# Reordering the first three blocks of a fused attention and expert kernel, and cutting its last tile in three

## The chip, the cores and the metric

The kernel runs on one core of a Trainium2 chip. The metric is the device time of one execution in microseconds (us), of the core that it runs on; medians of several executions are quoted. A trace's span, from the first to the last instruction, is about 1.8 us shorter than that time. "TensorE" does matrix multiplies, "VectorE" (DVE in the profile) and "ScalarE" (ACT) work on vectors, "GpSimd" (POOL) issues most loads here, and the sync engine (SP) issues the output transfers and the transposes by DMA. In profile lines PE is TensorE, PEld its weight loads, and a q after an engine's name marks its queue, which waits and issues transfers.

## The reference

```python
# q, k, v: (8, 8, 576, 64); attention within chunks of 64 positions
scores = scale * q_c @ k_c.T          # per chunk
attn = exp(scores - max) / (sum + 1e-9)
x = (attn @ v_c)                      # -> 4608 tokens x 512
h = x @ w_in                          # 512 x 2048
g = h * sigmoid(beta * h)
out = g @ w_out                       # 2048 x 512, float32
```

The kernel works on "units" of 256 tokens for attention and "blocks" of two units (512 tokens) for the two large products. Block 0 is units 0 and 1, block 1 is units 2 and 3, and so on.

## The kernel before

For each unit: block transposes of q and k (`emit_T`), scores and exp (`emit_sc`), values (`emit_pv`), norms (`emit_norm`: a reciprocal and a multiply on VectorE), and a transpose of x for the next product, by TensorE and a copy for units 0 to 5 (`emit_xt_pe`), by DMA from unit 6 on (`emit_xt_dma`). For each block: 16 hidden products (`emit_m`: four matmuls, tanh on ScalarE, gate product on VectorE) and four output tiles (`emit_t`: 16 matmuls, a copy on ScalarE, an output transfer). The engines keep to the order in which the program emits; the trace before shows it for VectorE, where unit 3's reciprocal starts at 48.45 us, behind the gate product of 48.11, though its matmuls started at 47.41 (unit 2's starts 0.37 after its own). PSUM is the memory that the kernel's matmuls write to. A tile takes one buffer of a pool there, called a bank here, and a bank goes to the next tile only when the tile that was in it has been read: in the trace before, unit 3's scores start at 45.37, after the copy that reads the tile in their bank has ended at 45.32.

In profile lines sc is a unit's scores, et their exp, rd and x the reciprocals and the values, xp the transposed x in PSUM and xt its copy; hps, sg and gt are a hidden product, its tanh and its gate product; ops and osb are an output tile in PSUM and its copy.

```python
ps_p = pool("ps_p", bufs=4, PSUM)   # one bank each: hidden products, output tiles, some x transposes
ps_s = pool("ps_s", bufs=1, PSUM)   # scores; second half of a unit's values
ps_x = pool("ps_x", bufs=1, PSUM)   # first half of a unit's values; x transposes
...
def emit_xt_pe(u, s):
    pool, tag = (ps_x, "x") if s == 0 else (ps_s, "s") if u == 2 else (ps_p, "p")
    ... four transposes into one bank, then nc.scalar.copy(out=xt_at(u, s), in_=xp)
...
for i in range(16):                       # block 0's output, units 2 and 3 between
    ...
    if i == 13:
        emit_xt_pe(2, 0); emit_xt_pe(2, 1)
    if i == 14:
        emit_sc(3, True)
    if i == 15:
        emit_m(1, 0, 0, 256)              # hidden product 0, unit 2's half
        emit_pv(3)
        emit_norm(3, 0); emit_norm(3, 1)
        emit_m(1, 1, 0, 256)
    emit_t(0, i % 4, 4 * (i // 4), 4 * (i // 4) + 4)
emit_xt_pe(3, 0); emit_m(1, 2, 0, 256)
emit_xt_pe(3, 1); emit_m(1, 3, 0, 256)
for m in range(4, KFF):                   # whole-block products from 4 on
    emit_m(1, m)
    if m < 8:
        emit_m(1, m - 4, 256, 256)        # unit 3's halves of 0 to 3
    ...
```

The softmax here doesn't subtract the row's maximum and nothing guards it: scores larger than these inputs give would overflow.

## Time and profile before

| | before |
|---|---|
| time, median of 6 | 291.71 us (291.54 to 292.50) |
| span of the trace | 290.0 us |
| TensorE busy | 283.1 us, 98% |
| start of unit 2's value matmuls | 40.58 us |
| start of the last matmul | 286.41 us |

TensorE is the bound, so what matters is where it starts late. The last two rows frame a stretch of 245.83 us.

### The profile page before, as it was taken

The page shows a single profiled execution, that of the slowest core. Times are in us where ns is not written, and L with a number is a line of the kernel's source. Part 1 is how long each engine was busy: PE and PEld are TensorE (multiplying, and loading weights), DVE is VectorE, ACT ScalarE, POOL GpSimd, SP SyncE. Part 2 cuts the span into 40 slices and gives each one's busy share as a digit, 9 for nine tenths or more (in the row PEclk, how much of TensorE's full clock was granted, in tenths as well). Part 3 has the DMA queues.
Part 4 walks back from the last instruction along what each step waited for, and adds up shares of the span by engine and source line. Part 5 has one row for each costly group of instructions (what it writes and reads, how often), then busy time and mean ns, then how long its engine had stood idle before and what let it go on. Part 6 is the DMA issues. An engine that isn't in the chain of part 4 may idle for free.

```text
span 290.0 us, 6476 instructions
## 1 busy us (share of the span) xinstructions
PE 283.1 (98%) x2695; PEld 135.5 (47%) x2695; DVE 139.8 (48%) x252; ACT 146.0 (50%) x224; POOL 97.5 (34%) x126
## 2 busy tenths in 40 slices
PE   7999999999999999999999999999999999999995
PEld 2464445545544444444444444444444444444444
DVE  3477444687366644534454444445453636433300
ACT  3277318783456645454545554455445544444411
POOL 8864569379152985070717070000000000000000
PEclk9999999999999999999999999999999999999999
DMA  9999999999969999999999999946346202100111
GB/s 143 170 196 205 177 176 212 211 161 158 133 98 135 200 168 144 168 151 156 135 123 171 118 158 113 198 65 92 91 107 78 75 36 72 38 36 36 38 72 72
DMA packets 141932, 36.86 MB, mean 127 GB/s; under 512 B 130000, under 2 KB 137424, under 8 KB 141904
## 3 DMA queue, kind: packets, MB, share of 16 engines
q0 software_dynamic: 101216, 18.10, 84.2%
q1 hardware_dynamic: 40544, 18.24, 34.4%
q8 instruction: 21, 0.34, 0.5%
q10 hardware_dynamic: 144, 0.13, 0.1%
q14 instruction: 7, 0.06, 0.1%
HBM read 36.71 MB, written 9.44 MB: 159 GB/s over the span
## 4 chain that ended last, share of the span: by engine, by line
PE 91%; DMA 2%; ACT 2%; DVE 2%; POOL 1%; issue 1%; DVEq 0%; ACTq 0%; POOLq 0%
PE hps L303 43%; PE ops L335 41%; DMA ku<-in_k_dram 2%; PE x L256 2%; PE sc L231 2%; PE sc L218 1%; PE ops L540 1%; ACT xt L288 1%; DVE x L271 1%; ACT sg L313 1%; PE warm L352 1%; POOL h L360 1%; PE xp L287 1%; DVE kT L154 0%; ACT osb L345 0%
## 5 line engine op out<-in xcount | busy, mean ns | idle before, releaser
L317 DVE SCALAR_TENSOR_TENSOR gt<-sg,hps 128x512 f16<-128x512 f32 (+1 forms) x152 | 99.2, 658 | 114.5 <-ACT sg L313 114.4
L313 ACT ACTIVATE sg<-hps,beta 128x512 f32<-128x512 f32 (+1 forms) x152 | 100.4, 665 | 74.7 <-PE hps L303 74.7
L303 PE MATMUL hps<-xt,win 128*128 128x512 f16 (+1 forms) x608 | 136.7, 368 | 0.4 <-ACT xt L288 0.2
L335 PE MATMUL ops<-wout,gt 128*128 128x512 f16 x560 | 131.1, 379 | 0.0
L303 PEld LDWEIGHTS <-win 128*128 128x128 f16 x608 | 57.6, 98 | 61.8 <-issue 0.9
L335 PEld LDWEIGHTS <-gt 128*128 128x128 f16 x560 | 53.8, 98 | 63.3
L345 ACT ACTIVATE osb<-ops 128x512 f32<-128x512 f32 x35 | 20.9, 598 | 44.4 <-PE ops L335 44.4
L110 POOL DMA_DIRECT2D vbig<-in_v_dram x40 | 34.2, 876 | 10.0 <-DMA wout<-in_moe_w_out_dram 4.3
L96 POOL DMA_DIRECT2D qu<-in_q_dram x22 | 18.7, 860 | 41.5 <-DMA qT<-qu 39.0
L271 DVE TENSOR_TENSOR x<-x,rd 128x512 f16<-128x512 f32 (+1 forms) x40 | 25.2, 637 | 1.4
L96 POOL DMA_DIRECT2D ku<-in_k_dram x22 | 18.8, 876 | 0.4 <-DMA ku<-in_k_dram 0.4
L240 ACT ACTIVATE et<-sc 128x1024 f16<-128x1024 f32 (+1 forms) x9 | 7.4, 834 | 10.2 <-PE sc L231 10.2
L352 PE MATMUL warm<-idle 128*128 128x512 f16 x39 | 11.2, 429 | 1.2 <-DVE braw L356 1.2
L267 DVE RECIPROCAL rd<-x 128x8 f32<-128x8 f32 x36 | 7.2, 200 | 8.8 <-PE x L256 8.8
L224 ACT ACTIVATE et<-sc 128x1024 f16<-128x1024 f32 x10 | 10.2, 1015 | 0.0
L256 PEld LDWEIGHTS <-et 64*64 64x64 f16 x576 | 6.1, 107 | 7.4 <-issue 3.8
L102 POOL DMA_DIRECT2D ku<-in_k_dram x10 | 7.7, 772 | 2.5 <-DMA win<-in_moe_w_in_dram 1.3
L102 POOL DMA_DIRECT2D qu<-in_q_dram x10 | 7.7, 781 | 2.4 <-DMA win<-in_moe_w_in_dram 1.4
L288 ACT COPY xt<-xp 128x512 f16<-128x512 f16 x12 | 6.7, 588 | 3.3 <-PE xp L287 3.3
L256 PE MATMUL x<-vbig,et 64*64 64x65 f16 x576 | 8.1, 195 | 0.0
L154 DVE STREAM_TRANSPOSE kT<-ku 128x512 f32<-128x512 f32 x7 | 5.0, 711 | 4.9 <-DMA ku<-in_k_dram 4.9
L553 DVE TENSOR_SCALAR osb<-ops 128x256 f32<-128x256 f32 x1 | 0.4, 424 | 12.5 <-PE ops L540 12.5
(34 smaller groups left out, 60.2 us busy)
## 6 DMA issues: line engine op xcount, KB each, us to landing
out_dram<-osb SPq DMA_DIRECT2D x35, 256.0 KB, 3.2
vbig<-in_v_dram POOLq DMA_DIRECT2D x32, 128.0 KB, 7.9
qu<-in_q_dram POOLq DMA_DIRECT2D x20, 128.0 KB, 6.6
ku<-in_k_dram POOLq DMA_DIRECT2D x20, 128.0 KB, 8.2
win<-in_moe_w_in_dram POOLq DMA_DIRECT2D x8, 256.0 KB, 9.2
wout<-in_moe_w_out_dram POOLq DMA_DIRECT2D x4, 512.0 KB, 12.2
qu<-in_q_dram POOLq DMA_DIRECT2D x4, 256.0 KB, 6.5
ku<-in_k_dram POOLq DMA_DIRECT2D x4, 256.0 KB, 7.3
```

The source lines that it names most:

```text
L96: nc.gpsimd.dma_start(out=tv[off:off + n, sp], in_=src[b, :, s:s + n, :].rearrange("h p d -> p h d"),)
L102: nc.gpsimd.dma_start(out=t[off // 2:(off + n) // 2], in_=src[b, :, s:s + n, :].rearrange("h (p r) d -> p h r d", r=2),)
L110: nc.gpsimd.dma_start(out=vbig[off:off + n, i, :, 0:D], in_=v[b, :, s:s + n, :].rearrange("h p d -> p h d"),)
L224: nc.scalar.activation(out=et, in_=sc, func=ACTF.Exp, scale=scale)
L256: nc.tensor.matmul(out=x[64 * c:64 * c + 64, r, g, 0:D + 1], lhsT=(et[64 * r:64 * r + 64, s, 4 * c + g, :] if u < XU else et[64 * r:64 * r ...
L271: nc.vector.tensor_tensor(out=o, in0=x[:, r, :, 0:D], in1=rd[:, r].to_broadcast(list(o.shape)), op=ALU.mult)
L303: nc.tensor.matmul(out=hps[:, 0:n], lhsT=w_in16[m // 2][:, kk, (m % 2) * 128:(m % 2) * 128 + 128], rhs=xr[:, c0 // CH:(c0 + n) // CH, 2 * ...
L313: nc.scalar.activation(out=sg[:, 0:n], in_=hps[:, 0:n], func=ACTF.Tanh, scale=beta2[:, m:m + 1])
L317: nc.vector.scalar_tensor_tensor(out=gt_t[j][:, m, c0:c0 + n], in0=sg[:, 0:n], scalar=1.0, in1=hps[:, 0:n], op0=ALU.add, op1=ALU.mult,)
L335: nc.tensor.matmul(out=ops, lhsT=gt_t[j][:, kk, t * 128:(t + 1) * 128], rhs=w_out16[kk // 4][:, kk % 4, :], start=(kk == 0), stop=(kk == K ...
L345: nc.scalar.activation(out=osb, in_=ops, func=ACTF.Copy, scale=0.5)
L352: nc.tensor.matmul(out=d[:, 0:w], lhsT=idle[:, 0:128], rhs=idle[:, 0:w])
```

## The change

Five edits, called by letters from here on. The intent is to take away TensorE's waits in the early blocks, where attention is still prepared by TensorE, VectorE and ScalarE, and to shorten the tail.

```diff
 # A: unit 2's x transposed into one bank, one copy
-                emit_xt_pe(2, 0)
-                emit_xt_pe(2, 1)
+                emit_xt_pair(2)       # 8 transposes into one ps_x bank, one 1024-column copy
 # B: the gate product behind unit 3's norms
-                emit_m(1, 0, 0, 256)
+                a0, v0 = emit_m(1, 0, 0, 256, True)
+                a0()
                 emit_pv(3)
                 emit_norm(3, 0)
                 emit_norm(3, 1)
+                v0()
 # C: a first half of product 4 moved up
-        for m in range(4, KFF):
+        emit_m(1, 4, 0, 256)
+        for m in range(5, KFF):
             emit_m(1, m)
-            if m < 8:
-                emit_m(1, m - 4, 256, 256)
+            if m < 10:
+                emit_m(1, m - 5, 256, 256)
 # D: unit 5's block transposes behind unit 4's norms
         emit_pv(4)
-        emit_T(5)
         emit_norm(4, 0)
         emit_norm(4, 1)
+        emit_T(5)
 ...                                  # and unit 5's scores and values one half tile later
 # E: the last output tile in pieces of 256, 128 and 128 columns, not two of 256
-        for hf in range(2):
+        for c0, n in ((0, 256), (256, 128), (384, 128)):
 ...                                  # VectorE copies the first and third, ScalarE the second
```

More of the change, by code (lines that the diff above doesn't have):

```diff
@@ L288, in emit_xt_pe, with emit_xt_pair @@
         nc.scalar.copy(out=xt_at(u, s), in_=xp)
+    def emit_xt_pair(u):
+        xp = ps_x.tile([128, 2, 4, 128], FP16, tag="x", name="xp")
+        for s in range(2):
+            xf = x16_t.pop((u, s)).rearrange("p r h d -> p (r h d)")
+            for g in range(4):
+                nc.tensor.transpose(out=xp[:, s, g, :], in_=xf[:, g * 128:(g + 1) * 128], identity=ident)
+        xt_at(u, 0)
+        j, o = unit_block[u]
+        nc.scalar.copy(out=xt_t[j][:, 2 * o:2 * o + 2], in_=xp)
     def emit_xt_dma(u, s):
@@ L467 @@
         emit_xt_pe(4, 1)
+        emit_t(1, 1, 0, 8)
         emit_sc(5)
-        emit_t(1, 1, 0, 8)
+        emit_t(1, 1, 8)
         emit_pv(5)
@@ L473 @@
         emit_T(7)
-        emit_t(1, 1, 8)
         emit_t(1, 2, 0, 8)
@@ L540 @@
                 nc.tensor.matmul(
-                    out=ops[:, 0:256],
+                    out=ops[:, 0:n],
                     lhsT=gt_t[NB - 1][:, kk, 384:512],
-                    rhs=w_out16[kk // 4][:, kk % 4, 256 * hf:256 * hf + 256],
+                    rhs=w_out16[kk // 4][:, kk % 4, c0:c0 + n],
                     start=(kk == 0),
@@ L547 @@
             osb = osb_p.tile([128, DM], FP32, tag="osb", name="osb")
-            dst = out[NT - 128:NT, 256 * hf:256 * hf + 256]
-            if hf == 0:
-                nc.scalar.activation(out=osb[:, 0:256], in_=ops[:, 0:256], func=ACTF.Copy, scale=0.5)
-                nc.sync.dma_start(out=dst, in_=osb[:, 0:256])
-            else:
-                nc.vector.tensor_scalar(out=osb[:, 0:256], in0=ops[:, 0:256], scalar1=0.5, scalar2=None, op0=ALU.mult)
-                nc.scalar.dma_start(out=dst, in_=osb[:, 0:256])
+            dst = out[NT - 128:NT, c0:c0 + n]
+            if c0 == 256:
+                nc.scalar.activation(out=osb[:, 0:n], in_=ops[:, 0:n], func=ACTF.Copy, scale=0.5)
+            else:
+                nc.vector.tensor_scalar(out=osb[:, 0:n], in0=ops[:, 0:n], scalar1=0.5, scalar2=None, op0=ALU.mult)
+            (nc.scalar if c0 == 384 else nc.sync).dma_start(out=dst, in_=osb[:, 0:n])
 _INS = ['q', 'k', 'v', 'moe_w_in', 'moe_w_out', 'moe_beta']
```

## The prediction

> **What bounds the kernel now.** I read the page first, for the share of each engine.
>
> ```profile
> PE 283.1 (98%) x2695; PEld 135.5 (47%) x2695; DVE 139.8 (48%) x252; ACT 146.0 (50%) x224; POOL 97.5 (34%) x126
> ```
>
> TensorE is busy 98% of 290.0 us, and the page shows it at full clock in every slice. A change that leaves its work alone can only win what TensorE waits, and the time before its first and after its last matmul. So next I read the waits of TensorE:
>
> ```profile
> PE xp L287 <- DVE x L271: 0.4, 2, 0.2
> PE sc L231 <- ACT xt L288: 0.3, 1, 0.3
> PE hps L303 <- ACT xt L288: 0.2, 1, 0.2
> ```
>
> These three rows are what this change aims at, 0.9 us in all, but they are too small. The profile models the end of a matmul well after the next could have started (379 ns for a 512-column matmul, though they start 216 ns apart), so part of each wait counts as busy. I therefore take waits from starts, in the timeline of the stage around unit 3:
>
> ```profile
> 44.00 1.03 PE L335 MATMUL ops<-wout,gt 128*128 128x512 f16 x4
> 44.25 1.07 ACT L288 COPY xt<-xp 128x512 f16<-128x512 f16 x2
> ...
> 45.37 0.70 PE L231 MATMUL sc<-qT,kT 32*64 32x64 f16 x64 [0.34 <-ACT xt L288]
> ...
> 48.11 0.42 DVE L317 SCALAR_TENSOR_TENSOR gt<-sg,hps 128x256 f16<-128x256 f32 x1 [3.73 <-ACT sg L313]
> ...
> 48.45 0.20 DVE L267 RECIPROCAL rd<-x 128x8 f32<-128x8 f32 x1
> 48.68 0.69 DVE L271 TENSOR_TENSOR x<-x,rd 128x512 f16<-128x512 f32 x1
> ...
> 49.30 0.60 ACT L345 ACTIVATE osb<-ops 128x512 f32<-128x512 f32 x1 [0.39 <-PE ops L335]
> ...
> 49.43 0.40 PE L287 MATMUL xp<-ident,x 128*128 128x128 f16 x4 [0.17 <-DVE x L271]
> 49.52 0.69 DVE L271 TENSOR_TENSOR x<-x,rd 128x512 f16<-128x512 f32 x1
> ...
> 49.86 0.58 ACT L288 COPY xt<-xp 128x512 f16<-128x512 f16 x1
> ...
> 50.27 0.40 PE L287 MATMUL xp<-ident,x 128*128 128x128 f16 x4
> ...
> 51.35 4.92 PE L303 MATMUL hps<-xt,win 128*128 128x512 f16 x28 [0.25 <-ACT xt L288]
> ```
>
> The reader is to see four late starts. Four output matmuls from 44.00 are through at 44.87 (4 x 0.216); with 0.09 for a change of tile shape (below) unit 3's scores could start at 44.96; they start at 45.37, as their bank holds unit 2's second transpose until its copy is read out: **0.41**. The four output matmuls at 48.24 are through at 49.10; unit 3's first transpose starts at 49.43: **0.33**. The four hidden products from 49.66[...] end at 50.10; the second transpose starts at 50.27: **0.17**. The four from 50.50 end at 50.94; the first whole-block product starts at 51.35, waiting for the second copy of x: **0.41**. Together 1.32 us. One more is in unit 4's stage:
>
> ```profile
> 65.72 0.70 DVE L154 STREAM_TRANSPOSE kT<-ku 128x512 f32<-128x512 f32 x1
> ...
> 66.35 0.67 DVE L154 STREAM_TRANSPOSE qT<-qu 128x512 f32<-128x512 f32 x1
> ...
> 66.94 0.17 DVE L267 RECIPROCAL rd<-x 128x8 f32<-128x8 f32 x1
> ...
> 67.99 0.69 DVE L271 TENSOR_TENSOR x<-x,rd 128x512 f16<-128x512 f32 x1
> ...
> 68.73 0.40 PE L287 MATMUL xp<-ident,x 128*128 128x128 f16 x4 [0.21 <-DVE x L271]
> ```
>
> VectorE does unit 5's block transposes before unit 4's norms. The second transpose of x could start at 68.36 (68.14 + 4 x 0.056) and starts at 68.73: **0.37**. From there to 286 us the chain of waits is unbroken matmuls. The tail:
>
> ```profile
> 283.03 3.66 PE L540 MATMUL ops<-wout,gt 128*128 128x256 f16 x32
> ...
> 286.78 0.42 DVE L553 TENSOR_SCALAR osb<-ops 128x256 f32<-128x256 f32 x1 [12.51 <-PE ops L540]
> ```
>
> After the last matmul come a 0.42 us copy, the DMA issue at 287.23, and its landing; the span ends at 290.0.
>
> [...] eight transposes from 43.56 to 44.00 are 55 ns apart though each has its own weight load, and 12 output matmuls from 40.96 to 43.56 take 216 ns each. [...] the reciprocal at 48.45 stands behind a gate product that waits for a tanh, though its matmuls started at 47.41. [...] In the chain of waits eight output matmuls take 1.73 us alone and 1.83 with such a change. The change moves these borders; their number stays. [...] here a 1024-column exp takes 1.015.
>
> **The change part by part.** Times below are on the clock of the kernel before. No matmul is added in count of columns, so the sum is waits removed.
>
> *Unit 2's x in one bank.* Eight transposes now fill the bank that has no part in unit 3's scores. Those need only unit 2's norm read out (42.04 + 0.69 = 42.73) and unit 3's block transposes (43.71 + 0.67 = 44.38), both before 44.96. So 0.41 goes. One 1024-column copy (estimate 1.02, from the exp) replaces two that took 1.07: nothing on the path. Unit 3's value matmuls move from 47.41 to 47.00; they need the exps, which end 1.08 after about 45.80, at 46.88: just in time.
>
> *Gate product behind unit 3's norms.* With VectorE free, the reciprocal starts 0.37 after the value matmuls start, as for unit 2 (40.58 to 40.95), and the second x is ready 1.78 after that (40.95 to 42.04 + 0.69): at 47.37 and 49.15, in place of 50.21. TensorE gets to the first transpose at 48.71 and needn't wait (0.33 gone). The second it reaches at 49.37, but that takes the bank of the fourth output tile, which ScalarE empties from 48.89 to 49.49, so it starts at 49.54.
>
> *A product's first half moved up.* ScalarE, in order, is what remains: output copy, x copy, tanh, x copy. Before, this ran from 49.30 to 51.30. It now starts 0.41 to 0.45 earlier, as the output matmuls do, and ends near 50.88; the first whole-block product can start near 50.92, not 51.35 (0.43). In front of it there is now one half-product more, 4 x 0.109 = 0.43, which before came after. So this stage gains 0.43 + 0.43 = **0.86** of its 1.32; 0.46 stays as a wait for the last copy of x. [...]
>
> *Unit 5's block transposes behind unit 4's norms.* The reciprocal can start at 66.02 + 0.37 = 66.39 and the second x is ready at 68.17, ahead of 68.36: **0.37** gained. The block transposes (1.4) then end near 69.5; unit 5's scores, moved behind eight output matmuls, start near 70.4. Unit 5's own x has less cover, 8 output matmuls where it had 16: ready 2.15 after its value matmuls start, wanted 0.38 + 0.09 + 1.73 + 0.22 = 2.42 after. No new wait.
>
> *Last tile in three pieces.* TensorE: 16 x 0.109 + 32 x 0.056 = 3.53 for 3.51, a loss of 0.02. [...] **0.15** together.
>
> Sum: 0.86 + 0.37 + 0.15 = 1.38 us. I take back 0.1 for rival A and get 291.77 - 1.28 = 290.5.
>
> **The rivals.** *A: given back at a transfer.* Block 3's first product at 99.00 reads x transposed by DMA, issued until 94.99 (92.36 + 2.63), with 2.4 to 7.5 us to landing in the view of that tile. TensorE gets there some 1.2 us earlier; the transposes mostly shift along, but unit 9's loads are now issued behind later block transposes and may crowd them. For it: DMA queues are over 90% busy there. Against: GpSimd was issuing unit 8's loads until 68.25 anyway, so the delay is a fraction of 1 us. Worth 0 to 0.6, then 290.4 to 291.0. [...] *C: all waits of unit 3's stage vanish* (ScalarE keeps up): 0.46 more, 290.0. Against it: four ScalarE operations in order stand between the output matmuls and the product.
>
> **Range and chances.** Predicted 290.5 us. Low 290.0 is rival C, high 291.1 is A in full[...]; the runs before spread 0.5 us. Faster by 2% would be under 285.9, and all waits and the tail of this kernel don't hold that; slower by 2% needs a stall of 6 us that nothing here suggests.
>
> **What the profile after would show.** Unit 3's scores start about 0.96 after the output matmuls ahead of them, not 1.37, with no wait on a copy. The reciprocal of unit 3 starts within 0.4 of its value matmuls, ahead of the gate product. TensorE's wait for a copy of x ahead of the first whole-block product stays, at 0.3 to 0.5. No wait at unit 4's second transpose. The last 16 matmuls start 55 ns apart[...]. I am wrong if a wait shows near block 3's first product, if the small pieces run slower, or if the first-block wait is gone.

Its sum came to 0.86 + 0.37 + 0.15 = 1.38 us, less 0.1 for rival A, which gives 1.28 and so 290.5. Of the tail's 0.15 only the loss of 0.02 on TensorE can be followed. "Such a change", beside the 1.73 and 1.83 us, is the change of tile shape. In the trace before, it shows at the scores that follow transposes as well: these are 56 ns apart, and from the last of them to the first score matmul it is 149 ns, 0.09 us more.

## The result

| | before | after |
|---|---|---|
| time, median | 291.71 us (6 runs) | 290.31 us (6 runs, 289.81 to 290.68) |
| ratio | | 0.9945 (0.9929 to 0.9961) |
| span of the trace | 290.0 us | 288.9 us |
| stretch from unit 2's values to the last matmul | 245.83 us | 245.07 us |
| from the last matmul's start to the end | 3.55 us | 3.15 us |

A ratio is the mean time of one kernel's fast runs over that of the other's of the same rounds, so it isn't quite the ratio of the medians. The medians differ by 1.40 us, which is within the 2% that counts as the same time, and the interval of the ratio excludes 1.

The page of the kernel after, engines' busy time, and then the one row that still stands among TensorE's waits past the first 10 us:

```profile
PE 282.7 (98%) x2715; PEld 136.0 (47%) x2715; DVE 139.9 (48%) x254; ACT 145.8 (50%) x224; POOL 97.5 (34%) x126
```

```profile
PE hps L313 <- issue: 0.3, 1, 0.3
```

The three rows that the prediction showed are gone. The row that came in their place will turn out to be a wait for a transfer. In the timeline of the stage around unit 3, after (columns: start us, us, engine, line, operation, tiles, and in brackets the idle time before):

```profile
44.11 1.03 PE L345 MATMUL ops<-wout,gt 128*128 128x512 f16 x4
...
45.06 0.71 PE L231 MATMUL sc<-qT,kT 32*64 32x64 f16 x64
...
47.11 0.45 PE L256 MATMUL x<-vbig,et 64*64 64x65 f16 x32
...
47.49 0.21 DVE L267 RECIPROCAL rd<-x 128x8 f32<-128x8 f32 x1 [3.43 <-PE x L256]
...
47.94 1.03 PE L345 MATMUL ops<-wout,gt 128*128 128x512 f16 x4
...
48.80 0.39 PE L287 MATMUL xp<-ident,x 128*128 128x128 f16 x4
...
49.00 0.60 ACT L355 ACTIVATE osb<-ops 128x512 f32<-128x512 f32 x1 [0.39 <-PE ops L345]
49.02 0.60 PE L313 MATMUL hps<-xt,win 128*128 128x256 f16 x4
49.18 0.74 DVE L327 SCALAR_TENSOR_TENSOR gt<-sg,hps 128x256 f16<-128x256 f32 x2
...
49.64 0.38 PE L287 MATMUL xp<-ident,x 128*128 128x128 f16 x4
```

This trace runs 0.10 us late at unit 2's values, so 0.10 is to be taken off each start to compare. Unit 3's scores then start at 44.96, 0.95 after the output matmuls ahead of them and with no wait for a copy, the reciprocal stands 0.38 behind the value matmuls (which start at 47.11) and ahead of the gate product, and the first transpose, at 48.80, follows its four output matmuls (47.94 + 4 x 0.216) at once. The second still does. The four products at 49.02 (109 ns from start to start) are through at 49.46, and it starts at 49.64, 0.18 late, just after the output copy ends at 49.60: it waits for that tile's bank. The chain of waits after, in order of time, shows what is left behind it (columns: start us, us, what):

```profile
49.00 0.25 ACT osb L355
...
49.49 0.58 ACT xt L288
...
50.33 0.61 ACT xt L288
...
50.97 10.98 PE hps L313 x60
```

ScalarE, in its order, is the path from 49.00 to 50.93: output copy, x copy, tanh, x copy. The half products behind the second transpose, the last of them the one moved up, are done by 50.73, and the first whole-block product starts at 50.97, so 0.24 is lost. The stage's 1.32 us of waits became 0.42.

Unit 4's stage after:

```profile
65.59 0.21 DVE L267 RECIPROCAL rd<-x 128x8 f32<-128x8 f32 x1 [0.59 <-PE x L256]
...
67.28 0.70 DVE L154 STREAM_TRANSPOSE kT<-ku 128x512 f32<-128x512 f32 x1
67.33 0.61 PE L287 MATMUL xp<-ident,x 128*128 128x128 f16 x8
```

The norms come first, and the eight transposes of x run as one group: the 0.37 is gone. The tail after:

```profile
282.27 3.70 PE L552 MATMUL ops<-wout,gt 128*128 128x256 f16 x48
...
286.07 0.29 DVE L564 TENSOR_SCALAR osb<-ops 128x128 f32<-128x128 f32 x1 [1.42 <-PE ops L552]
286.39 0.37 ACTq L565 DMA_DIRECT2D out_dram<-osb  x1
```

The 48 matmuls take 3.70 us where 32 took 3.66; in the trace the last 32 start 55 to 56 ns apart. The last copy takes 0.29 us, and the last transfer, of 64 KB, lands 1.59 us after its issue starts, where that of 128 KB took 1.75.

The two stages thus gained 0.90 and 0.37, and the new last tile lengthens the stretch by 0.10 (3.48 from its first matmul's start to its last's, for 3.38); yet the stretch got only 0.76 shorter. The other 0.4 is lost at block 3's first product:

```profile
96.08 1.89 PE L345 MATMUL ops<-wout,gt 128*128 128x512 f16 x8
...
98.25 1.02 PE L313 MATMUL hps<-xt,win 128*128 128x512 f16 x4 [0.28 <-issue]
```

The output matmuls ahead are through at 97.81, and this product starts at 98.25, 0.44 late. The profile names no releaser, but the second transpose by DMA of unit 7's x, which it reads, landed at 98.16 in this trace, 0.09 before the start. In the kernel before it landed at 98.48 and the product started at 99.00 with no wait:

```profile
99.00 1.03 PE L303 MATMUL hps<-xt,win 128*128 128x512 f16 x4
```

### The profile page after: what moved, and what is told of

The parts are those of the page before. It is cut to its first block, busy times and chain, and to the rows that moved or that the text cites. A ratio compares the mean times of both kernels' runs of the same rounds, so it can differ in the third digit from the quotient of the medians.

```text
span 288.9 us, 6524 instructions
## 1 busy us (share of the span) xinstructions
PE 282.7 (98%) x2715; PEld 136.0 (47%) x2715; DVE 139.9 (48%) x254; ACT 145.8 (50%) x224; POOL 97.5 (34%) x126
## 4 chain that ended last, share of the span: by engine, by line
PE 94%; DMA 2%; ACT 1%; issue 1%; DVE 1%; POOL 0%; DVEq 0%; ACTq 0%; POOLq 0%
PE hps L313 43%; PE ops L345 42%; PE x L256 2%; DMA h<-in_k_dram 2%; PE warm L362 2%; PE sc L231 2%; PE sc L218 1%; PE ops L552 1%; ACT xt L288 1%; PE xp L287 1%; ACT sg L323 0%; POOL h L370 0%; DVE x L271 0%; DVE t L177 0%; PE xp L295 0%
## 5 line engine op out<-in xcount | busy, mean ns | idle before, releaser
L288 ACT COPY xt<-xp 128x512 f16<-128x512 f16 x10 | 5.7, 588 | 3.8 <-PE xp L287 3.8
L564 DVE TENSOR_SCALAR osb<-ops 128x256 f32<-128x256 f32 (+1 forms) x2 | 0.7, 358 | 12.1 <-PE ops L552 12.1
```

## The experiments

Two theories were open. **Theory 1:** TensorE now comes so early that x by DMA is late as a rule, and a third of the gain is given back (rival A of the prediction). **The rival:** that one landing was chance, and the gain is the sum of the waits taken away. Beside this I wanted each edit's own worth, since four edits of one stage could hide each other. The table has what was measured; the stage is the distance from the start of unit 2's to that of unit 4's value matmuls, and all four columns of lengths, in us, are from the one profiled execution of each kernel. Each ratio is to the kernel before in the same rounds, whose medians were 291.71, 291.77, 291.87 (one run, beside the single runs but the last) and 292.04 us.

| kernel | stage | stretch | last matmul to end | wait at block 3 | time, median (runs) | ratio to before |
|---|---|---|---|---|---|---|
| before | 25.44 | 245.83 | 3.55 | 0 | 291.71 (6) | |
| after | 24.53 | 245.07 | 3.15 | 0.44 | 290.31 (6) | 0.9945 |
| after, again | 24.54 | 244.64 | 3.15 | 0 | 290.54 (5) | 0.9953 (0.9941 to 0.9965) |
| A, B, C | 24.54 | 244.93 | 3.55 | 0 | 291.42 (5) | 0.9981 (0.9969 to 0.9993) |
| D | 25.44 | 245.45 | 3.55 | 0 | 291.26 (5) | 0.9980 (0.9968 to 0.9993) |
| E | 25.45 | 245.93 | 3.16 | 0 | 292.07 (4) | 0.9999 (0.9982 to 1.0015) |
| A | 25.04 | 245.43 | 3.56 | 0 | 291.65 (1) | |
| B | 25.37 | 245.76 | 3.56 | 0 | 291.76 (1) | |
| C | 25.05 | 245.55 | 3.55 | 0.11 | 291.75 (1) | |
| A, C | 24.64 | 245.04 | 3.55 | 0 | 291.16 (1) | |
| first try at cover | 24.54 | 248.71 | 3.16 | 0 | 294.53 (6) | 1.0094 (1.0076 to 1.0113) |
| second try at cover | 24.54 | 244.64 | 3.15 | 0 | 290.31 (5) | 0.9943 (0.9931 to 0.9956) |
| after, two moves at unit 3 | 24.18 | 244.28 | 3.16 | 0 | 290.57 (1) | |
| both together | 24.18 | 244.28 | 3.15 | 0 | 289.76 (5) | 0.9925 (0.9913 to 0.9937) |

**The changed kernel again, unaltered.**

> The changed kernel unaltered, for a second trace. Theory 1 (TensorE now arrives before block 3's x, which comes by DMA and did not move along): a gap of 0.3 to 0.6 us ahead of block 3's first product (about 98 us) again, as the 0.44 us of the first trace. Rival (chance of that one execution): TensorE reaches it with no gap, or a gap below 0.1. Time 290.0 to 290.6 either way.

There is no wait at block 3. The timeline of this run:

```profile
96.38 1.89 PE L345 MATMUL ops<-wout,gt 128*128 128x512 f16 x8
...
98.10 1.03 PE L313 MATMUL hps<-xt,win 128*128 128x512 f16 x4
```

Eight output matmuls at 216 ns end at 98.10, and the product follows at once; x had landed at 96.98. Of the eleven traces in which this product stands where it did before, two show a wait, 0.44 and 0.11, and the second of these is a kernel with edit C alone; there too the product starts 0.09 after x lands (98.93 and 99.02). So Theory 1 falls as a rule: it is the scatter of a transfer's landing, 5.54 us after its issue in the first trace of the changed kernel and 4.07 in this one. The evidence is one trace for each kernel, and only three of the eleven have TensorE as early as the changed kernel does; one of these three waits. What remains true is that there is little slack: where nothing waits, x lands between 0.37 and 1.23 us before the product starts, 0.52 in the trace before.

**An output tile ahead of block 3's first product, first try.** Half an output tile stands ahead of that product; putting the other half there too would give x 1.73 us more to land.

```diff
-                    items.append((0.98 * (t + 0.5 * hf) / 4, 1, ("t", t, hf)))
+                    at = 0.01 if (j, t, hf) == (3, 0, 1) else 0.98 * (t + 0.5 * hf) / 4
+                    items.append((at, 1, ("t", t, hf)))
```

> The changed kernel with one move: the second half of block 2's first output tile (8 matmuls, 1.73 us) goes ahead of block 3's first product. Theory 1: the gap at block 3's first product is gone and the time is 0.3 to 0.5 us under the changed kernel's, near 289.9. Rival (no gap as a rule): same time within 0.1. Second rival (the wait only moves, to unit 8's scores or values): the gap turns up within 5 us after and the time stays.

It missed the theory and both rivals: 294.53 us. TensorE waits 1.66 us at 112.91 for unit 9's scores, and again 0.98 and 1.43 at 130 and 161. The sync engine's own rows, first of this kernel and then of the changed one again, tell why:

```profile
100.65 0.33 SPq L357 DMA_DIRECT2D out_dram<-osb  x1
101.15 1.87 SPq L149 DMA_TRANSPOSE kT<-ku  x1
```

```profile
94.27 1.25 SPq L149 DMA_TRANSPOSE kT<-ku  x1
```

The output transfer of the tile, now finished early, came into the sync queue ahead of unit 9's block transposes, and the queue issues nothing from 94.10 to 100.65, waiting for the tile. (In the trace after, the queue's waits at that line are put down to the tile's copy in 27 cases, 142.4 us in all.) The transposes were issued 6.88 us later, and q's landed at 112.77, right before the late scores. The chain of waits puts that wait down to a gate product that ended about then, which is a case of a wait for several things being given the wrong name. The two later waits I didn't trace to their releasers; they too are gone in the next run.

**The same cover, transposes first.** Unit 9's block transposes get the lowest key, so they stay ahead in the queue.

```diff
+            if j == 3:
+                items = [(-1,) + it[1:] if it[2] == ("T", 9) else it for it in items]
```

> As the first try at covering block 3's first product, but unit 9's block transposes stay ahead of the output transfer in the sync queue's order. Theory (that try lost its 4 us because the transposes waited behind an output transfer): no waits at unit 9's scores (112.9), 130 and 161 us, kT of unit 9 issued near 94 us, time 290.0 to 290.5. Rival (the order of matmuls itself was at fault): a wait of over 0.5 us after 100 us remains.

As the theory said: no wait after 100 us, and kT of unit 9 issued at 93.86. The stretch, 244.64, is that of the changed kernel without its unlucky landing, so the order of matmuls was not at fault. The cover itself wins nothing that these runs could show.

**Edits A, B and C alone**, and **edit D alone.**

> Kernel before with the three edits around unit 3 alone (pair in one bank, late gate product, half product moved up). Theory: starts in the trace show 0.9 us of waits gone there, 0.4 left (bank of the second transpose 0.18, copy of x 0.24); ends in a time 0.9 us under before if block 3's x still comes in time, and 0.5 if TensorE now waits for it. Rival: scores and copies trade places and under 0.4 us is won.

> Kernel before with the block transposes behind unit 4's norms alone. Theory: the 0.37 us gap at unit 4's second transpose is gone and, TensorE being only 0.37 us earlier, block 3's x comes just in time (it had about 0.4 us to spare): time 0.3 to 0.4 under before. Rival: unit 9's later loads make block 3's x late and the 0.37 comes back as a gap near 99 us: time within 0.1 of before.

A, B and C take 0.90 from the stage, all of the changed kernel's gain there, and D takes 0.38 from the stretch. Of the times, 0.9981 and 0.9980 are each about 0.5 us of gain with an interval of some 0.35 on either side: right in sign, too coarse for more. The 0.9 that was expected of A, B and C in the time doesn't show there; it rests on the trace.

**One edit at a time around unit 3** (each is its part of the diff above).

> Kernel before with unit 2's x in one bank alone. Measured from the start of unit 2's value matmuls to the start of the last matmul (245.83 us before), which leaves out the scatter of the first 40 us. Theory (a chain of ScalarE work that starts with unit 3's fourth output tile moves along): 0.41 less, the waits 0.33, 0.17 and 0.41 after it unchanged. Rival (the waits behind it grow): under 0.2 less.

> Kernel before with the late gate product alone. Theory: the 0.33 us wait at unit 3's first transpose goes, but ScalarE's order (output copy, x copy, tanh, x copy) still starts at the same output tile, so the wait for the last copy of x grows from 0.41 to about 0.8 and only 0.05 to 0.1 is won on that stretch. Rival (the norms were the bound): 0.33 to 0.5 won.

> Kernel before with the half product moved up alone. Theory: it fills the 0.41 us wait for the last copy of x with 0.43 us of work that came later; 0.40 to 0.44 won, no wait left there. Rival (the copy itself comes later, as ScalarE has the extra tanh): under 0.2 won.

> The first and third edit without the late gate product. Theory: 0.84 won on the stretch, against 0.90 with all three, so the late gate product is worth 0.06 although it takes away two waits of 0.50. Rival (its 0.33 is real): 0.5 to 0.6 won.

A wins 0.40 and C 0.39. B wins 0.07, though its own wait is gone. In the chain of waits of the kernel with B alone:

```profile
49.37 0.25 ACT osb L345
...
49.86 0.58 ACT xt L288
...
50.69 0.61 ACT xt L288
...
51.34 3.73 PE hps L303 x21
```

ScalarE's sequence starts with the same output tile as before, since that tile's matmuls wait for nothing that B moves. Its end moved by 0.07 us only, so TensorE reached the whole-block product earlier and waited there 0.68 us in place of 0.41. With A and C but not B, the waits of 0.33 and 0.17 for the norms are both still there and the wait for the copy is nil; B on top of that wins 0.10 (0.06 was expected). The waits of this stage are thus not a list to be added up: A and C shorten the path, and B mostly moves a wait from one place on it to another.

**Edit E alone.**

> Kernel before with the last tile in three pieces alone. Theory: from the start of the last matmul to the end 3.15 us instead of 3.55, the last 32 matmuls 55 to 56 ns apart, the stretch up to the last matmul the same but for 0.07 more; time 0.3 under before. [...]

From the last matmul's start to the end it is 3.16, not 3.55, and the stretch is 0.10 longer, so the trace shows a net 0.29. The time shows nothing (0.9999): in this trace unit 2's values started 0.66 later than in that of before, and the ratio's interval is 0.5 us to either side. For E I rely on the trace.

**The two waits left at unit 3.** If ScalarE's order is the path, the last copy should come ahead of the tanh, and the transpose should use a bank that is already free.

```diff
-        pool, tag = (ps_x, "x") if s == 0 else (ps_s, "s") if u == 2 else (ps_p, "p")
+        pool, tag = (ps_x, "x") if s == 0 else (ps_s, "s") if u == 3 else (ps_p, "p")
...
-        emit_m(1, 2, 0, 256)
+        a2, v2 = emit_m(1, 2, 0, 256, True)
         emit_xt_pe(3, 1)
+        a2()
+        v2()
```

> The changed kernel with the two moves at unit 3 alone (bank and place of the copy). Theory: unit 2's to unit 4's value matmuls 24.15, 0.35 to 0.4 less; a gap near 98 us may or may not show, as the DMA lands with scatter. Rival: under 0.1 won.

> The changed kernel with three more moves: unit 3's second transpose into the bank that its own norm has freed, its copy ahead of the tanh of the product between, and block 3's first product behind one whole output tile, with unit 9's block transposes still issued ahead of that tile's output transfer. Theory: the two waits left at unit 3 (0.18 and 0.24) fall to 0.05 or less, 0.35 to 0.4 won from unit 2's to unit 4's value matmuls (24.54 to about 24.15), no gap near 98 us, and a time 0.4 to 0.6 under the changed kernel's, 289.8 to 290.1. Rival (the copy's place was not the bound): the stretch stays within 0.1 of 24.54.

The stage falls to 24.18 in both, 0.36 less, and a 0.06 wait is left. In the timeline of the kernel with everything:

```profile
49.15 0.39 PE L287 MATMUL xp<-ident,x 128*128 128x128 f16 x4
49.18 1.07 ACT L288 COPY xt<-xp 128x512 f16<-128x512 f16 x2
49.37 3.91 PE L313 MATMUL hps<-xt,win 128*128 128x256 f16 x25
```

The two copies run back to back, and TensorE goes on. This kernel's median is 289.76 us (289.58 to 289.92), ratio 0.9925: below the kernel before, and below the changed kernel too. The fairest comparison is with the second try at cover, which ran beside it on the same chip and has the changed kernel's stage and stretch: 290.10 to 290.43, with no run in common. Of the 0.57 between the spans of these two traces, 0.36 is stretch and 0.21 an earlier start. The run with the two moves alone is a single time, 290.57, in a trace whose start was 1.0 us later than that of the full version, so it doesn't contradict this.

## Why the prediction was right

The time, 290.31, lies within the range and 0.2 from the predicted 290.5, and the mechanism held. Point by point:

- **Unit 3's stage, 0.86:** measured 0.90 or 0.91 in every trace that has A, B and C as they are. A was put at 0.41 and gave 0.40, C at 0.43 and gave 0.39 alone. The wait that was to stay, 0.46 for the last copy, is 0.18 + 0.24 = 0.42. The prediction put all 0.46 down to the copy, though by its own working the second transpose waits from 49.37 to 49.54 for a bank; that wait is the 0.18, with the bank that was named, and the copy's own 0.24 is under the 0.3 to 0.5 that was written for it. That B removes 0.33 of wait and hardly any time follows from the working, where ScalarE's sequence starts with the output tile; the runs with B alone and without B show it.
- **Unit 4's stage, 0.37:** measured 0.38, with no new wait at unit 5.
- **The tail, 0.15, was mis-sized:** it is 0.29 net. The copy is 0.13 shorter (0.424 to 0.291 us). The matmuls lose 0.05, not 0.02: 0.10 from first start to last, of which the shorter last matmul gives 0.05 back (3.49 was to be taken for the tile before, by the same sum, not 3.51). The landing is 0.16 shorter (1.75 to 1.59 us). Some 0.06 more came at the end, where one wait fewer follows the last landing; I hadn't counted it. Why the count of those last waits differs was not tested.
- **Rival A, for which 0.1 was taken back:** it showed in 2 of 11 traces. In the first, 0.44 was lost; so one of the signs by which the prediction called itself wrong, a wait near block 3's first product, was there in that trace and not in the second. The reason given, unit 9's later loads, is not supported: those loads ended at 78.69 us in the trace after and at 79.85 in that before. The landings in the traces point to the loads that come next, unit 10's, issued 6 to 10.5 us before that transpose of x. In all 14 traces x lands 1.4 to 2.0 us after the last of them, and the two go together: 9.68 us from issue to landing for that load and 5.54 for x in the first trace of the changed kernel, 8.64 and 4.07 in the second, with a correlation of 0.95 over the 14. Whether these loads hold x up, and why they scatter, was not tested.
- **Rival B, slower small pieces:** the last 32 matmuls start 55 to 56 ns apart. **Rival C, no waits left:** it did not happen with this change. The two moves above reach it.

Together, 0.90 + 0.38 + 0.29 is 1.57 us, and the trace of the changed kernel without the unlucky landing has it: 244.64 + 3.15 is 1.59 less than 245.83 + 3.55. Less the occasional wait at block 3, that fits the 1.40 between the medians and the 1.2 of the second comparison (291.77 to 290.54). The predicted 1.28 is nearer to these than its parts are: the tail gave 0.14 more than was written, and the first trace lost 0.44 where 0.1 was taken back.

## What to carry to other kernels

Follow a wait to what starts the sequence that ends it: a wait removed in front of an engine that is bound to another engine's order can move on and win little, as B's did: 0.33 us of wait gone, 0.07 won. Before moving a piece of work, look at what it puts into every in-order queue: the first cover cost 4 us through an output transfer ahead of two transposes. And where a gain is smaller than the scatter of the program's start, 1.0 us here, measure it between two points inside the trace.
